# A decode step of two layers on one core: gate by three ScalarE functions, K slots freed by halves, a V head kept, priorities per batch

## The chip, the cores and the metric

One core of a Trainium2 chip. The metric is the device time of one execution of the whole program, in microseconds. Times on the chip come from the program's runs; the profile is one profiled execution.

## The reference, cut to what matters

```python
x = A_x                                            # [4, 1, 512], bf16
x = x + attention(layernorm(x), k_cache, v_cache, wq, wo)
x = x + ffn(layernorm(x), w_gate, w_up, w_down)
x = x + attention(layernorm(x), k_cache, v_cache, wq, wo)   # the same caches and weights again
x = x + ffn(layernorm(x), w_gate, w_up, w_down)

def attention(x, k_cache, v_cache, wq, wo):        # caches [4 batches, 8 heads, 4096, 128]
    q = (x @ wq)                                   # 32 query heads, 4 to a K/V head
    p = softmax(q @ k.T * 128 ** -0.5)
    return (p @ v) @ wo
def ffn(x, w_gate, w_up, w_down):                  # 512 -> 1792 -> 512
    return (gelu_tanh(x @ w_gate) * (x @ w_up)) @ w_down
```

All tensors are bf16. K and V are 32 heads each of 4096 x 128, 1.05 MB a head; the weights are some 13.9 MB. Both layers use the same caches and weights.

## The kernel before, in words

The two layers are called L = 0 and L = 1, the batches b = 0 to 3. The batches are independent of each other until the last step, so the kernel goes through the batches one after the other and does both layers of a batch on one load of its K heads. The weights are loaded once and stay in SBUF.

**Slots.** K and V heads come into `KV`, a tile of `SLOTS` = 12 slots, each for one head (128 partitions x 8 KB) or for two halves. Near the end the four parts of `wq_sb` serve as four more slots. A K head occupies its slot until the scores of layer 1 have used it. A V head is loaded once for each layer, except where `HELD` keeps it: for batches 1 to 3 head 7 stays from layer 0 to layer 1. The V loads of layer 1 go by halves (`HALVES`, 512 KB each), so that half a slot can be filled as soon as half a head has been used; a half is read by one of the two `values` steps of the head. K heads are loaded whole, and their slots come free when both halves of the scores are done.

**The steps of one batch.** K heads are transposed in place: heads 5 and 7 (`BY_PE`) by TensorE into `R_ps` with a copy by ScalarE (`kturn`, `kcopy`), the others by VectorE (`turn`, L366, two halves a head). `expand` (L392) spreads q into the weights `Qb`; `scores` (L415) makes the scores of four heads (z = 0 or 1) in two halves m of 16 matmuls; `top`, `bias`, `expo`, `pturn`, `pswap`, `pcopy` make the softmax's weights; `values` (L485) multiplies half a head of V, 16 matmuls; `oscale` scales. For layer 0 the dense chain of the batch follows: `outproj` (`proj`, `half_out`, `half_sum` L639, `proj_last` L623), `addback` (L646, L647), the norm (`ln_sq` L500, `ln_mm` L506, `ln_mid`, `ln_var`, `ln_root`), gate and up matmuls (`up`, L655), their transpose (`ffturn`, L662), the gate (`gelu_a`, `gelu_b` L688, `gelu_y`, `gelu_c` L705 to L707), `down` (L715), `addback`, the norm, and the q projection for layer 1 (`qmm` L538, `qevac` L551, `qturn` L556, `qsplit` L595, `qrep` L605). Only then can layer 1's scores of this batch run. The output projection of layer 1 is done once, for all four batches, after the last V head, and with the second FFN it makes the tail: `leave` (L732) adds and sends the output off.

The norm's factor 1/root is not applied to the norm's output but later: to q in the exponent's scale, and in the FFN to the gate's argument and to the product.

**The order.** `Plan` holds every step as a node with its engine, an estimated duration and what it depends on. `run` goes through time as a list scheduler: for each engine it takes the step that can begin first, with some `PATIENCE` for one of higher level that is ready a little later. The level is the longest path to the end, plus an offset by the kind of step (`LEAD`, `stage`). The loads go out on SP's queue in a fixed order: x, wq, K of batch 0, half of wo, V of batch 0, the rest of wo, w_gate, w_up, w_down, then for each batch b from 1 on K(b), V(b) for layer 0, V(b-1) for layer 1. Each waits on SP for a slot that its readers have left, and what stands behind it on SP waits too. `warm` puts filler matmuls (`spin`, L1004) before steps of TensorE that begin after an idle time. The whole order is computed when the program is built; on the chip nothing is chosen.

## Time and profile before

| | |
|---|---|
| time, median of 3 runs | 292.3 us (291.77 to 293.2) |
| the profiled execution's own time | 291.89 us |
| its span, first to last instruction | 290.1 us |
| granted clock of TensorE | 0.998 |
| busy: PE, DVE, ACT | 236.3, 133.5, 74.5 us |
| loaded by the load queue | 111.42 MB |

The page and the views give times in us from the span's start. L715 is line 715 of the kernel before. A row of a group or of the timeline has the engine, what is written and read, the shapes and how often; a row of the windows has the stretch, the busy time of each engine, the granted clock, the share of the sixteen DMA engines' time that packets took (over 1 where packets of one engine overlap) and the rate.

### The profile page before, as it was taken

What the parts mean: (1) busy time and instruction counts of PE and PEld (TensorE: products, weight loads), DVE (VectorE), ACT (ScalarE), POOL (GpSimd) and SP (SyncE); (2) the same over time, 40 slices, a digit from 0 to 9 for tenths busy, and PEclk for the clock granted to TensorE, in tenths of its full rate; (3) what the DMA queues carried; (4) which work ended last, traced back from release to release, by engine and by line L of the source; (5) the groups of instructions that cost most, each with busy time, mean ns of one, the idle gap of its engine ahead of it and who ended that gap; (6) DMA issues with size and microseconds to landing.
All of it is one profiled execution on the core that took longest, in us unless ns stands there. A gap on an engine that the chain in (4) does not pass through costs nothing.

```text
span 290.1 us, 9733 instructions
## 1 busy us (share of the span) xinstructions
PE 236.3 (81%) x4419; PEld 138.3 (48%) x4419; DVE 133.5 (46%) x380; ACT 74.5 (26%) x167; POOL 0.7 (0%) x6
## 2 busy tenths in 40 slices
PE   4988887878687888798888698879977889897794
PEld 1433454443233565455434465554445655565552
DVE  4149911002289942052389721343998213444034
ACT  1020751001023852101224731000338321113010
POOL 0000000000000000000000000000000000000000
PEclk9999999999999999999999999999999999999999
DMA  7999999999999999999999999999999999999910
GB/s 312 412 421 419 376 405 416 414 371 426 415 407 395 419 421 417 402 407 406 393 417 416 425 416 411 405 407 390 413 422 416 408 387 403 396 382 420 411 47 1
DMA packets 21657, 112.04 MB, mean 386 GB/s; under 512 B 2032, under 2 KB 6128, under 8 KB 12272
## 3 DMA queue, kind: packets, MB, share of 16 engines
q1 hardware_dynamic: 21568, 111.42, 95.3%
q8 instruction: 34, 0.56, 0.8%
q14 instruction: 7, 0.06, 0.0%
q10 hardware_dynamic: 48, 0.01, 0.0%
HBM read 111.42 MB, written 0.00 MB: 384 GB/s over the span
## 4 chain that ended last, share of the span: by engine, by line
DMA 62%; PE 16%; SPq 11%; DVE 7%; issue 2%; ACT 1%; DVEq 0%
DMA KV<-in_A_v_cache_dram 43%; DMA KV<-in_A_k_cache_dram 8%; SPq L351 7%; PE O_ps L485 7%; DMA wd_sb<-in_B_w_down_dram 6%; DMA wq_sb<-in_A_v_cache_dram 5%; SPq L741 3%; PE S_ps L415 3%; DVE KV L366 2%; PE R_ps L715 1%; PE R_ps L538 1%; DVE PA L662 1%; PE S_ps L1004 1%; PE R_ps L655 1%; DVE sm L421 1%
## 5 line engine op out<-in xcount | busy, mean ns | idle before, releaser
L485 PE MATMUL O_ps<-PA,KV 128*128 128x56 bf16 x1920 | 66.3, 188 | 20.8 <-DMA KV<-in_A_v_cache_dram 17.3
L485 PEld LDWEIGHTS <-KV 128*128 128x128 bf16 x1920 | 57.6, 97 | 40.8 <-DMA KV<-in_A_v_cache_dram 32.4
L1004 PE MATMUL S_ps<-iden_b 128*128 128x512 bf16 x226 | 67.7, 401 | 3.6 <-DVE iden_b L321 3.6
L366 DVE STREAM_TRANSPOSE KV<-KV 128x1024 int32<-128x1024 int32 x48 | 56.5, 1214 | 0.6 <-DMA KV<-in_A_k_cache_dram 0.4
L379 ACT ACTIVATE KV<-R_ps 128x512 bf16<-128x512 f32 x64 | 34.9, 595 | 28.0 <-PE R_ps L373 27.9
L415 PE MATMUL S_ps<-KV,PA 128*32 128x512 bf16 x384 | 35.3, 394 | 2.1 <-DVE KV L366 1.3
L1004 PEld LDWEIGHTS <-iden_b 128*128 128x128 bf16 x227 | 21.9, 107 | 27.6 <-issue 11.7
L373 PE MATMUL R_ps<-iden_b,KV 128*128 128x128 bf16 x256 | 22.1, 219 | 6.3 <-ACT KV L379 3.1
L421 DVE TENSOR_REDUCE sm<-S_ps 128x1 f32<-128x512 f32 x16 | 10.8, 677 | 27.4 <-PE S_ps L415 27.4
L373 PEld LDWEIGHTS <-KV 128*128 128x128 bf16 x256 | 15.8, 97 | 14.8 <-issue 10.2
L415 PEld LDWEIGHTS <-PA 128*32 128x32 bf16 x384 | 11.4, 94 | 13.2 <-issue 4.4
L493 DVE TENSOR_TENSOR OT<-O_ps,XS 128x4 bf16<-128x4 f32 (+1 forms) x12 | 2.0, 164 | 32.9 <-PE O_ps L485 32.9
L415 PE MATMUL S_ps<-KV,QN 128*32 128x512 bf16 x128 | 16.8, 381 | 0.2 <-ACT KV L379 0.2
L438 ACT ACTIVATE PA<-S_ps,sm 128x512 bf16<-128x512 f32 x16 | 11.7, 732 | 20.4 <-DVE sm L432 17.6
L632 ACT ACTIVATE PA<-R_ps 128x256 f32<-128x256 f32 x10 | 3.8, 384 | 46.2 <-PE R_ps L613 41.1
L529 ACT ACTIVATE sm<-sm 128x1 f32<-128x1 f32 (+1 forms) x10 | 2.0, 203 | 52.6 <-DVE sm L522 52.6
L493 DVE TENSOR_TENSOR OT<-O_ps,rdk 128x16 bf16<-128x16 f32 (+3 forms) x18 | 3.1, 170 | 26.7 <-PE O_ps L485 26.7
L463 ACT ACTIVATE PA<-T_ps 128x512 bf16<-128x512 f32 x16 | 9.6, 597 | 13.0 <-PE T_ps L455 11.8
L556 DVE STREAM_TRANSPOSE PA<-PA 128x256 int32<-128x256 int32 x10 | 4.4, 437 | 14.9 <-ACT PA L551 14.2
L613 PE MATMUL R_ps<-wo_sb,OT 128*1 128x512 bf16 (+1 forms) x124 | 8.7, 378 | 2.6 <-DMA wo_sb<-in_A_wo_dram 1.4
L646 DVE STREAM_TRANSPOSE PA<-R_ps 128x128 f32<-128x128 f32 x9 | 2.9, 317 | 16.5 <-PE R_ps L623 10.2
L447 DVE STREAM_TRANSPOSE PA<-PA 128x256 int32<-128x256 int32 x16 | 7.0, 434 | 7.5 <-ACT PA L438 7.5
(92 smaller groups left out, 173.9 us busy)
## 6 DMA issues: line engine op xcount, KB each, us to landing
KV<-in_A_v_cache_dram SPq DMA_DIRECT2D x34, 1024.0 KB, 15.0
KV<-in_A_k_cache_dram SPq DMA_DIRECT2D x32, 1024.0 KB, 13.5
KV<-in_A_v_cache_dram SPq DMA_DIRECT2D x46, 512.0 KB, 7.0
wq_sb<-in_A_wq_dram SPq DMA_DIRECT2D x1, 4096.0 KB, 12.2
wo_sb<-in_A_wo_dram SPq DMA_DIRECT2D x2, 2048.0 KB, 19.5
wq_sb<-in_A_v_cache_dram SPq DMA_DIRECT2D x4, 1024.0 KB
wg_sb<-in_B_w_gate_dram SPq DMA_DIRECT2D x1, 1792.0 KB
wu_sb<-in_B_w_up_dram SPq DMA_DIRECT2D x1, 1792.0 KB
```

The source lines that it names most:

```text
L351: nc.sync.dma_start(out=where[name], in_=src.rearrange("(p c) d -> p (c d)", p=P))
L366: nc.vector.transpose(out=w, in_=w)
L373: nc.tensor.matmul(R_ps[k % 2][:, P * u:P * u + P], lhsT=where[name][:, at:at + P], rhs=iden_b[:], start=True, stop=True)
L379: nc.scalar.activation(out=where[name][:, 512 * k:512 * k + 512], in_=R_ps[k % 2][:], func=ACT.Copy)
L415: nc.tensor.matmul(S_ps[z][32 * t:32 * t + 32], lhsT=w, rhs=k, start=(m == 0 and x == 0), stop=(m == 1 and x == 3))
L421: nc.vector.tensor_reduce(out=cms[:, z:z + 1], in_=S_ps[z][:].rearrange("p c r -> p (c r)"), axis=AX.X, op=ALU.max)
L438: nc.scalar.activation(out=PW[L][z].rearrange("p (a r e) -> p a r e", a=8, e=2), in_=S_ps[z][:].rearrange("p (a e) r -> p a r e", e=2), fu ...
L463: nc.scalar.activation(out=PW[L][z], in_=T_ps[z][:].rearrange("p t x -> p (t x)"), func=ACT.Copy)
L485: nc.tensor.matmul(Ov[L][:, j], lhsT=vw[:, c, :], rhs=w[:, c // 2, :, c % 2].unsqueeze(1).broadcast_to([P, WIDE, 4]), start=(m == 0 and c ...
L613: nc.tensor.matmul(R_ps[0][32 * i:32 * i + nb, :], lhsT=src[:, 4 * j + i, 0:nb], rhs=wo_sb[:, 4 * j + i, :], start=(first and j == heads[0 ...
L741: return lambda pick: nc.sync.dma_start(out=dst, in_=src.rearrange(pat, q=P))
L1004: nc.tensor.matmul(sinks[place].rearrange("p (a n) -> p a n", a=4), lhsT=iden_b[:], rhs=every, start=True, stop=True)
```

## The change

It has these parts:

- **V head 7 of batch 0 is kept** from layer 0 to layer 1 as in the other batches (`HELD`), and its two half loads of layer 1 are gone.
- **K slots come free by halves.** The two halves of a slot have readers of their own, for whole loads too: the first half of a K head is free after `scores` m = 0. K head 3 of batch 1 (`K_HALVES`) is loaded in two halves into the two halves of one slot.
- **Gate.** 1/(1 + e^u) was made by exp on ScalarE, then an add and a reciprocal on VectorE; now ScalarE does exp, ln(1 + .) and exp of the negative.
- **Norm.** The sums of x and of x² are two matmuls instead of one, so that the mean's doesn't wait for the squares.
- **q of layer 1, first half.** The matmuls write their columns in another order (`qmm_apart`), and VectorE transposes 512 fp32 columns in PSUM in place (`qturn_apart`) instead of ScalarE's copy and a bf16 transpose in SBUF.
- **The end.** The gate's matmuls and their transpose go in two parts of 8 and 6 of the 14 chunks (`CUT`, also for w_down's loads); the norm's factor is applied to the product's last rows in `leave` (`last_root`, `rrow`) and no more to the product; heads 4, 5, 6 are scaled one by one, and heads 5 and 6 take the narrow path of `proj_last`.
- **Order.** `LEAD` gets an offset for each batch and kind, `PATIENCE` depends on the kind of step, and some estimated durations change.

```diff
-HELD = ((), (7,), (7,), (7,))
-HALVES = {(b, 1, j) for b in range(3) for j in range(8)} | {(3, 1, 6)}
+HELD = ((7,), (7,), (7,), (7,))
+HALVES = {(b, 1, j) for b in range(3) for j in range(7)} | {(3, 1, 6)}
+K_HALVES = {(1, 3)}
-PATIENCE = (0.5, 1.5, 0.7)
-LEAD = {"tn1": -3, "val0": 1, "sc10": -2, "chain": 2, "sc11": -6, "sm00": 1, "os0": -6, "op": -2, "sm01": 11, "sm10": 10, "qx1": 4, "other": 5, "sc00": 2, "sm11": 8, "os1": -4, "tn0": -2, "sc01": 1}
+PATIENCE = (0, 11.7, 5.1, 7.5, 0)
+LEAD = {"chain": (26.5, 10.5, 23.5, 46.5), "end": (-35, -36.5, -45.5, -72), "kt1": (3.5, -7, -16.5, 24),
...
+        "sm11": (1, 15, 57.5, 62), "tn0": (-47.5, -37, -37.5, -45.5), "tn1": (-60.5, -107.5, -79, -91),
+        "val0": (-95.5, -54.5, -70.5, -63.5), "val1": (0, 13, 33.5, -23)}
-WARM = 0.45
+WARM = 0.4
...
                 if v["readers"] is not None:
-                    slot_rd[pick] = v["readers"]
+                    mate = pick
                     whole[pick[0]] = not v["half"]
-                    if not v["half"]:
-                        slot_rd[pick[0], 1] = v["readers"]
+                    if v["half"]:
+                        slot_rd[pick] = v["readers"]
+                    else:
+                        slot_rd[pick[0], 0], slot_rd[pick[0], 1] = v["readers"]
...
+    def ln_place(s, nb):
+        return O_ps[0][:, 512 - CD * nb:] if s else R_ps[1][:, 0:CD * nb]
+
+    def ln_mm(s, bs, nb):
+        def emit():
+            st = ln_place(s, nb).rearrange("p (k b) -> p k b", k=CD)
+            nc.tensor.matmul(st, lhsT=ones_mean, rhs=XS[:, s, :, bs], start=True, stop=True)
+        return emit
...
+    def qturn_apart():
+        nc.vector.transpose(out=R_ps[0][:], in_=R_ps[0][:])
...
+    def last_root():
+        nc.vector.scalar_tensor_tensor(out=junk, in0=rs, scalar=1.0, in1=pick_b, op0=ALU.mult, op1=ALU.mult,
+                                       accum_out=rrow)
...
             nc.scalar.activation(out=u, in_=u, func=ACT.Exp, scale=-2.0 * GELU_C * GELU_A)
+            nc.scalar.activation(out=u, in_=u, func=ACT.Ln, bias=1.0)
+            nc.scalar.activation(out=u, in_=u, func=ACT.Exp, scale=-1.0)
...
             else:
-                nc.vector.tensor_tensor(out=g, in0=g, in1=y.unsqueeze(1).broadcast_to([P, CF, nb]),
-                                        op=ALU.mult)
                 nc.vector.tensor_tensor(out=g, in0=g, in1=d, op=ALU.mult)
...
-    def gelu_c(nb):
-        def emit():
-            d, g, u, h = ff(nb)
-            nc.vector.tensor_scalar(out=u, in0=u, scalar1=1.0, scalar2=1e30, op0=ALU.add, op1=ALU.min)
-            nc.vector.reciprocal(out=u, in_=u)
+    def gelu_h(nb):
+        def emit():
+            _, g, u, h = ff(nb)
             nc.vector.tensor_tensor(out=h, in0=g, in1=u, op=ALU.mult)
...
-        nc.vector.tensor_tensor(out=yo, in0=xrow, in1=R_ps[0][:, 0:P], op=ALU.add)
+        nc.vector.scalar_tensor_tensor(out=yo, in0=R_ps[0][:, 0:P], scalar=rrow, in1=xrow, op0=ALU.mult, op1=ALU.add)
...
-            g = [[7], [6, 5, 4], [3, 2, 1, 0]] if b < B - 1 else [[0], [1, 2, 3], [7], [4, 5], [6]]
+            g = [[7], [6, 5, 4], [3, 2, 1, 0]] if b < B - 1 else [[0], [1, 2, 3], [7], [4], [5], [6]]
...
+            rd = [[("sc", b, 1, j // 4, m)] for m in range(2)]
+            if (b, j) in K_HALVES:
+                for m in range(2):
+                    if j >= 3:
+                        soft = [("sc", b - 1, 1, 0 if j < 7 else 1, m)]
+                    pl.load(name + (m,), 4.15, ld_part(name, m, src), rd[m], soft=soft, half=True)
+            else:
+                pl.load(name, 8, ld_head(name, src), rd, soft=soft)
...
-        a = add(("lnq", tag), "DVE", 0.17, [after], ln_sq(bs, nb))
-        a = add(("lnm", tag), "PE", 0.4, [a], ln_mm(bs, nb), ins=4)
-        a = add(("lnc", tag), "DVE", 0.37, [a], ln_mid(bs, nb))
-        v = add(("lnv", tag), "DVE", 0.33, [a], ln_var(nb))
+        s = add(("lnq", tag), "DVE", 0.17, [after], ln_sq(bs, nb))
+        m = add(("lnm", tag), "PE", 0.35, [after], ln_mm(0, bs, nb), ins=4)
+        a = add(("lnc", tag), "DVE", 0.3, [m], ln_mid(bs, nb))
+        s = add(("lns", tag), "PE", 0.35, [s, m], ln_mm(1, bs, nb), ins=4)
+        v = add(("lnv", tag), "DVE", 0.45, [s, a], ln_var(nb))
...
+            if not z and not root:
+                after = add(("qm", tag, z), "PE", 1.1, [after], qmm_apart(bs), ins=32)
+                last = add(("qt", tag, z), "DVE", 0.72, [after], qturn_apart)
+                last = spread_q(b, 1, z, last, "apart")
+                continue
...
+            for k in range(2):
+                u1 = add(("up", tag, 0, k), "PE", (0.55, 0.45)[k], [a, u1], up(0, wg_sb, bs, nb, k), ins=32)
+                t0 = add(("ft", tag, 0, k), "DVE", (0.44, 0.36)[k], [u1, t0], ffturn(0, k))
...
+    p, y = parts(B - 1, 1), rs
+    a = outproj(("op", "last"), p, len(p) - 2, 1, al, B, [dense_end], [])
+    r = add("rz", "DVE", 0.1, [("os", B - 1, 1, i) for i in range(len(groups(B - 1, 1)))], rows_clear)
+    w, a = a, ln(("f", "last"), a, al, B, y)
+    r = add("rp", "DVE", 0.2, [w, r], rows)
+    r = add("ro", "DVE", 0.45, [r, ("lnv", ("f", "last"))], rows_turn)
+    a = ffn("last", a, al, B, y)
+    y = add("rr2", "DVE", 0.16, [("lnr", ("f", "last")), ("gh", "last")], last_root)
+    add("out", "DVE", 0.32, [a, r, y], leave)
```

More of the change, by code (lines that the diff above doesn't have):

```diff
@@ L607, in qrep, with proj @@
         return emit
-    def proj(src, nb, heads, first, last):
+    def proj(src, cols, nb, heads, first, last):
         def emit():
@@ L616, in proj, with proj_last @@
         return emit
-    def proj_last(src, nb, heads, last):
+    def proj_last(src, cols, nb, heads, last):
         def emit():
```

184 lines of the change are left out of this document (100 added, 84 removed), and 4 rows, old and new, of the table LEAD.

## The prediction

> **What bounds the kernel now.** I read the page first (share of each engine, the DMA line, the sizes of the loads), then the stretches (busy time, DMA share and GB/s of chosen windows), then the DMA queue's waits and its timeline, and last the chain of waits for the two places where something other than the stream decides.
>
> ```profile
> PE 236.3 (81%) x4419; PEld 138.3 (48%) x4419; DVE 133.5 (46%) x380; ACT 74.5 (26%) x167; POOL 0.7 (0%) x6
> GB/s 312 412 421 419 376 405 416 414 371 426 415 407 395 419 421 417 402 407 406 393 417 416 425 416 411 405 407 390 413 422 416 408 387 403 396 382 420 411 47 1
> q1 hardware_dynamic: 21568, 111.42, 95.3%
> L1004 PE MATMUL S_ps<-iden_b 128*128 128x512 bf16 x226 | 67.7, 401 | 3.6 <-DVE iden_b L321 3.6
> KV<-in_A_v_cache_dram SPq DMA_DIRECT2D x46, 512.0 KB, 7.0
> ...
> 104.00:110.00 6.00, 4.91 (x112) 3.65 (x112) 1.13 (x2) 2.17 (x4) 0.00 (x0) 1.00 1.02 419
> 184.00:194.00 10.00, 8.50 (x251) 5.84 (x248) 4.71 (x22) 0.62 (x3) 0.00 (x0) 1.00 1.02 407
> ```
>
> PE is 81% busy, but 67.7 us of its 236.3 are L1004, the filler matmuls of `spin`; without them it works some 169 us of 290, and DVE and ACT less. The load queue moves 111.42 MB and keeps the sixteen engines at 95.3% of the span, and the GB/s line stays between 371 and 426 from the second slice to the 38th. So the stream of loads bounds the kernel: it ends near 276 us, and a tail of dependent steps follows. What a change is worth is bytes, gaps in the stream, and the tail. In a stretch of whole heads (1024 KB each) the stream runs at 419 GB/s, in one of half heads (512 KB) at 407, both at a DMA share of 1.02: halves cost 3% of rate and no idle time.
>
> The one gap lies between batch 0 and batch 1:
>
> ```profile
> 86.00:87.00 1.00, 1.00 (x26) 0.53 (x19) 1.00 (x2) 0.18 (x1) 0.00 (x0) 1.00 0.87 360
> 87.00:88.00 1.00, 0.94 (x5) 0.30 (x4) 0.90 (x6) 0.00 (x0) 0.00 (x0) 1.00 0.75 287
> 88.00:89.00 1.00, 0.28 (x5) 0.17 (x4) 0.68 (x3) 0.87 (x2) 0.00 (x0) 1.00 0.96 369
> ...
> 65.98 0.33 SPq L351 DMA_DIRECT2D KV<-in_A_k_cache_dram  x1
> KV<-in_A_k_cache_dram SPq DMA_DIRECT2D x1, 1024.0 KB, 23.3
> 86.42 3.08 SPq L351 DMA_DIRECT2D KV<-in_A_k_cache_dram  x4
> 84.39 2.02 PE L415 MATMUL S_ps<-KV,PA 128*32 128x512 bf16 x32 [0.21 <-DVE PA L392]
> ```
>
> The fourth K head of batch 1 is issued at 65.98 and lands 23.3 us later, at 89.3. The next load is issued at 86.42, when the 32 matmuls of layer 1's first scores (heads 0 to 3) end: only they free a slot. Three windows fall under 1.02 by 0.15, 0.27 and 0.06, so 0.48 us of stream is lost here.
>
> **The change part by part.**
>
> *Bytes.* V head 7 of batch 0 stays in its slot for both layers, so two half loads go: 1.05 MB at 407 GB/s = 2.58 us. K head 3 of batch 1 goes from 419 to 407: 1.05 x (1/407 - 1/419) = 0.07 us more. Net -2.5.
>
> *The gap.* The held head takes the slot that K head 3 had at 65.98, so only three K heads are queued ahead, and the stream runs dry 1.05 MB / 419 = 2.5 us earlier. Against that, halves of a slot are freed: K head 3's first half may go after 16 of the 32 score matmuls, 2.02 / 2 = 1.0 us earlier than 86.42. And the chain to these scores changes:
>
> ```profile
> 78.90 0.59 PE R_ps L715 x28
> 80.07 0.18 DVE XS L500
> 80.29 0.40 PE R_ps L506 x2
> 82.22 0.61 ACT PA L551
> 82.85 0.46 DVE PA L556
> 81.38 1.25 DVE L366 STREAM_TRANSPOSE KV<-KV 128x1024 int32<-128x1024 int32 x1
> ```
>
> It starts when w_down has landed (the bytes ahead of it are the same). Its last part has 24 matmuls instead of 28: 0.59 x 4/28 = -0.08. The mean's matmul no longer waits for the squares: from 80.29 to where the squares began, 80.07, -0.22; the second matmul and its reduction lie beside the q projection. For q's first half, ACT's copy and DVE's bf16 transpose (0.61 + 0.46 and a hop of 0.02) become one DVE transpose of 512 fp32 columns in PSUM. The tail's row at 282.79, quoted below, has 448 columns in 0.66, so an estimate is 0.75, and -0.34. Sum -0.64, if DVE is free: the K transpose of 81.38 ran to 82.63 under the cover of ACT's copy. The new transpose would be ready near 81.95; behind that K transpose it starts at 82.65, ends at 83.40 and not 83.31, and the three gains come to +0.1. I take -0.5, since the order is made anew from priorities that rank the chain over K transposes. So the refill comes 0.9 to 1.6 earlier than 86.42; I take 1.5, near 84.9.
>
> What that does to the stream's end: behind the refill stand the same bytes in both kernels (K head 3 has moved behind it, a V head has left). DMA engines that run dry in both kernels therefore end earlier by what the refill moved, 1.5; those that don't, by the full 2.5. The 0.48 us over two microseconds show that not all are dry at once; I take 7 in 10 for the new gap: 2.5 - 0.7 x (2.5 - 1.5) = 1.8. Bounds: 0.9 (all dry, no gain of the chain) and 2.5 (no further loss).
>
> The new wait stands on SP's queue: K head 3 waits there for the first half of the scores, and behind it K heads 4 to 7 and the V heads, which need these scores or later ones anyway. From its issue at 86.42 until the share is back at 0.96 pass 1 to 1.5 us. That delay is in both kernels and cancels; only if the second half, issued 1.0 after the first, leaves a hole of its own does it cost again (a rival below). The Trainium skill speaks against halving here: "DMA: Bandwidth & Descriptors", under "Anatomy of one DMA" (there for the GpSimd path), gives each DMA a fixed cost of about 2.0 us beside its bytes, which for one more DMA would turn the bytes' -2.5 into -0.5. At 184 to 194 us the trace does not show such a charge: other loads move meanwhile.
>
> *Slots later on.* Of the four slots freed by the last scores before 91.85, K head 7 takes one that a V head had; V head 3 of batch 1 follows on V head 7's last use, which layer 1 makes first. Batches 1 and 2 run so today, and their stretches show no gap like the one above. Cost 0, covered by some 5 us of loads in flight; thin, since the queue's waits have
>
> ```profile
> SPq L357 <- PE O_ps L485: 22.5, 27, 2.0
> ```
>
> 27 half loads that waited for PE to free a slot. Where a new order frees them late by more than is in flight, the stream loses it one for one: 0 to 2.5 us, nothing taken.
>
> *The dense chains of batches 1 to 3* shorten as batch 0's. They don't end the stream; 0. *The larger leads and patience* reorder PE, DVE and ACT; where the stream covers them, 0.
>
> *The tail* after the last landing is on the path:
>
> ```profile
> 278.46 0.34 PE R_ps L639 x4
> 278.80 0.54 PE O_ps L485 x16
> 279.73 0.29 PE R_ps L623 x16
> 280.68 0.17 DVE XS L500
> 280.97 0.41 DVE PA L728
> 281.81 0.96 PE R_ps L655 x16
> 282.79 0.66 DVE PA L662
> 284.05 0.22 DVE PA L681
> 284.26 0.56 DVE PA L662
> 284.82 0.11 DVE PA L697
> 284.95 0.22 DVE PA L699
> 285.17 0.12 DVE PA L705
> 285.31 0.52 DVE PA L706
> 285.85 0.23 DVE PA L707
> 286.12 0.98 PE R_ps L715 x56
> 287.12 0.29 DVE PA L732
> 284.30 0.25 ACT L688 ACTIVATE PA<-PA 128x56 f32<-128x56 f32 x1 [1.80 <-DVE PA L681]
> ```
>
> - Half sums: today L639 at 278.46 stands between the two halves of the last head. With heads 5 and 6 both in the last part they come earlier: 0 to -0.34, taken -0.2. Head 5's own 16 narrow matmuls (0.29 by L623) run before the last half lands.
> - Norm: the squares (0.17 and gaps, -0.2) leave the path, and the rows' transpose (280.97, 0.41) goes behind the variance, so that it doesn't take the place that the squares left.
> - Gate matmuls and transpose in two parts: the first part's transpose (256 of 448 columns, 0.38) runs beside the second part's matmuls; then 192 columns, 0.28, behind matmuls that end as before at 282.77 or 0.1 later for twice as many instructions. 0.66 becomes 0.3 to 0.5; -0.2.
> - Gate: today from ACT's start at 284.30 to the end of L707 at 286.08. After: ACT has three steps, 3 x 0.25 + 2 x 0.02 = 0.79, to 285.09; DVE beside it the second transpose to 284.82 and one product (0.22, L697 is gone) to 285.06. The last product then ends at 285.09 + 0.05 + 0.23 = 285.37: -0.71. The last root, one step on four columns, lies beside the 0.98 of L715, and L732's successor keeps its 0.29.
>
> The row of 0.25 is the price I use for each ACT step. The Trainium skill, "ScalarE: Activation LUTs", under "Rules for kernel authors", would budget about 0.3 us and 0.83 ns an element for each: 1.04 for three by my estimate, and the gate would bring 0.46. The row doesn't agree with it, by 0.1 a step.
>
> Sum of the tail: -0.2 - 0.2 - 0.2 - 0.7 = -1.3; from -0.7 (no gain from order and split, 0.5 from the gate) to -1.7.
>
> **Sum.** The profiled execution took 291.89 us (span 290.1), 0.4 under the median of 292.3. 291.89 - 1.8 - 1.3 = 288.8; its own bounds are 287.7 (2.5 and 1.7) and 290.3 (0.9 and 0.7). I forecast 288.8.
>
> **The rivals.**
>
> *The gap adds nothing.* The chain gains enough, or enough DMA engines are late, that all 2.5 arrives: 291.89 - 2.5 - 1.3 = 288.1. For it: the stream never fell under 0.75 in a window. Against it: 2.5 us less is queued, and the refill gains at most 1.6.
>
> *A later stall gives part back.* The waits above show V slots freed late in the half-head stretches; 1 to 2.5 us lost there gives 289.8 to 291.3.
>
> *Slower: K transposes ahead of the dense chain.* In batch 0, DVE has six transposes of 1.25 us for the three landed K heads (L366). If the new order puts them ahead of the chain to layer 1's scores, every microsecond by which the first half of those scores ends later than 85.4 moves the refill, and with it the stream's end. The change breaks even when the refill comes 1.3 us later than 86.42, the tail's gain; it is 0.5% slower from 1.3 + 1.5 = 2.8 us later, three of these transposes beyond the lost 1.0. With all six in front (7.5 us, less the 1.0): 291.89 + 6.5 - 1.3 = 297; with four 294.6. Against it: today one such transpose ran there, in a hole of the chain.
>
> *A hole between the halves.* The first half is 0.52 MB, 1.3 us at 407. If a load into a dry queue takes its 1 to 1.5 us anew and the second half comes late, the hole is up to 1.0: 289.8. The Trainium skill's fixed cost (above) would make it 2.0, and 290.8. Against it: the halves' issues lie 1.0 apart, less than 1.3.
>
> *The bytes don't count.* If something else than the stream held the end, only the tail's -1.3 is left: 290.6. The GB/s line speaks against it.
>
> **How the numbers follow.** A measurement of this kernel can tell about 0.5% from no change, 1.46 us: under 290.4 is faster, over 293.4 slower. The forecast has 0.49, the gap that adds nothing 0.16, the later stall 0.13, the hole 0.04, the slower order 0.10, the bytes that don't count 0.08. Faster: the first two whole, the hole, and 0.07 of the stall, 0.49 + 0.16 + 0.04 + 0.07 = 0.76. Same: 0.04 of the stall, the 0.08, and 0.01 of the slower order that stays small: 0.13. Slower: 0.09 of the order and 0.02 of a stall over 4 us: 0.11. The range leaves out the slower order and the far ends: 287.4 to 291.5; the likeliest case alone is 287.7 to 290.3.
>
> **What would show it.** Right: queue bytes down by 1.05 MB; a dip of the DMA share near 84 to 87 us, deeper than today's, with the next K load issued near 85; the stream's end 1.8 us earlier; from the last V matmul to L732's counterpart 1.1 us less; three ACT steps of about 0.25 in the gate. Wrong: the same end of the stream in spite of fewer bytes, a second dip after 100 us, K transposes on DVE between w_down's landing and the scores, or ACT steps over 0.4.

## The result, and the profile after

The changed kernel takes 295.08 us (median of 11 runs, 293.98 to 299.97), the kernel before 292.78 us in runs beside it. The ratio is 1.0093, interval [1.0065, 1.0120]: 0.9% or 2.7 us slower, where 3.1 us less were forecast. A few executions of either kernel are longer at a lower clock; the ratios leave them out and so are not quite the quotient of the medians. The profiled execution of the changed kernel took 297.44 us (span 295.6, granted clock 0.977), 2.4 over its median. So its trace shows where time goes; how much a part costs is taken from the ratios below.

The page of the kernel after; columns as before:

```profile
PE 233.0 (79%) x4428; PEld 142.8 (48%) x4428; DVE 133.5 (45%) x383; ACT 74.6 (25%) x173; POOL 0.7 (0%) x6
PEclk9999999999999979999999799999989999999979
GB/s 315 408 425 418 371 412 415 408 385 419 415 278 371 419 421 401 364 390 401 349 412 417 421 391 369 374 390 396 386 421 423 413 413 407 400 405 417 361 14 2
q1 hardware_dynamic: 21424, 110.37, 93.5%
L1078 PE MATMUL S_ps<-iden_b 128*128 128x512 bf16 x182 | 56.0, 412 | 3.6 <-DVE iden_b L343 3.6
```

The 1.05 MB are gone (110.37 against 111.42), and yet the stream ends later. Slice 12, at 81 to 89 us, fell from 407 to 278 GB/s: that is the forecast gap, but deeper. Slices 17 to 20 and 24 to 29 stand at 349 to 401, where before had 390 to 416: a second loss, a stall after 100 us. The clock row has four slices at 7 or 8 where before had none, and there are 182 fillers where there were 226.

How the stream falls behind is seen best by adding up the packets of the load queue in the trace: the time at which so many MB have arrived, in before, and by how much each kernel is later (one profiled execution each; labels as in the experiments).

| MB | before, us | after | e4 | e12 | e18 | e5 | e15 | e10 |
|---|---|---|---|---|---|---|---|---|
| 32 | 80.7 | 0.0 | 0.0 | 0.2 | 0.0 | 0.1 | 0.2 | 0.0 |
| 36 | 91.0 | 2.7 | 2.6 | 3.5 | 2.7 | 0.9 | 0.1 | 0.8 |
| 44 | 110.2 | 2.7 | 2.5 | 3.5 | 2.7 | 1.3 | 0.1 | 0.8 |
| 52 | 129.7 | 4.1 | 2.7 | 3.5 | 3.4 | 1.3 | 0.8 | 1.1 |
| 60 | 149.9 | 5.0 | 2.4 | 3.4 | 3.2 | 1.2 | 0.7 | 1.3 |
| 76 | 188.4 | 6.8 | 2.5 | 3.5 | 3.3 | 1.8 | 0.8 | 1.3 |
| 92 | 227.8 | 7.4 | 2.8 | 3.9 | 3.3 | 1.9 | 1.0 | 3.3 |
| 108 | 268.3 | 6.3 | 1.5 | 2.7 | 2.7 | 2.4 | 1.1 | 6.5 |

A kernel that keeps the head has 1.05 MB less to load in all, 2.5 us: with a lag of 2.5 it is level. After reaches that lag by 36 MB, in the gap behind batch 0, and loses some 4 us more between 44 and 76 MB. How much is lost there differs from trace to trace: summed in the same way, three other kernels with the new order (e17, e1, e8) lose 1.1, 1.4 and 2.0 us between 44 and 76 MB, and four with the old order and the kept head (e6, e18, e3, e7) 0.0, 0.6, 1.2 and 1.8. So the table shows where this execution lost its time; what a part costs is read from the ratios. Its last byte arrives at 281.83, before's at 278.00.

The profiled execution's 5.55 us over before are then: the last byte 3.83 later; from there to the transpose behind the last projection 4.16 instead of 2.12 (+2.04); from that transpose to the end of the last add 6.61 instead of 7.29 (-0.68); the way out +0.32; outside the span +0.05.

### The profile page after: what moved, and what is told of

It reads as the page before. It is cut to its first block, busy times and chain, and to the rows that moved or that the text cites. A ratio compares the mean times of both kernels' runs of the same rounds, so it can differ in the third digit from the quotient of the medians.

```text
span 295.6 us, 9761 instructions
## 1 busy us (share of the span) xinstructions
PE 233.0 (79%) x4428; PEld 142.8 (48%) x4428; DVE 133.5 (45%) x383; ACT 74.6 (25%) x173; POOL 0.7 (0%) x6
## 3 DMA queue, kind: packets, MB, share of 16 engines
q1 hardware_dynamic: 21424, 110.37, 93.5%
HBM read 110.37 MB, written 0.00 MB: 373 GB/s over the span
## 4 chain that ended last, share of the span: by engine, by line
DMA 59%; PE 22%; SPq 10%; DVE 5%; issue 3%; ACT 0%; DVEq 0%
DMA KV<-in_A_v_cache_dram 45%; PE O_ps L507 9%; DMA KV<-in_A_k_cache_dram 8%; SPq L373 6%; DMA wd_sb<-in_B_w_down_dram 6%; PE S_ps L437 6%; SPq L795 3%; PE R_ps L395 1%; DVE sm L443 1%; PE R_ps L662 1%; PE R_ps L708 1%; PE R_ps L767 1%; PE R_ps L578 1%; DVE PA L716 0%; ACT PA L485 0%
## 5 line engine op out<-in xcount | busy, mean ns | idle before, releaser
L507 PE MATMUL O_ps<-PA,KV 128*128 128x56 bf16 x1920 | 67.5, 191 | 17.6 <-DMA KV<-in_A_v_cache_dram 14.5
L507 PEld LDWEIGHTS <-KV 128*128 128x128 bf16 x1920 | 60.0, 98 | 34.9 <-DMA KV<-in_A_v_cache_dram 24.3
L1078 PE MATMUL S_ps<-iden_b 128*128 128x512 bf16 x182 | 56.0, 412 | 3.6 <-DVE iden_b L343 3.6
L388 DVE STREAM_TRANSPOSE KV<-KV 128x1024 int32<-128x1024 int32 x48 | 55.9, 1210 | 0.6 <-DMA KV<-in_A_k_cache_dram 0.5
L395 PE MATMUL R_ps<-iden_b,KV 128*128 128x128 bf16 x256 | 23.1, 228 | 10.1 <-DMA KV<-in_A_k_cache_dram 5.6
L1078 PEld LDWEIGHTS <-iden_b 128*128 128x128 bf16 x188 | 18.0, 107 | 23.5 <-issue 9.8
L395 PEld LDWEIGHTS <-KV 128*128 128x128 bf16 x256 | 17.0, 102 | 18.0 <-issue 9.8
L437 PEld LDWEIGHTS <-PA 128*32 128x32 bf16 x384 | 12.0, 94 | 16.6 <-issue 8.0
L515 DVE TENSOR_TENSOR OT<-O_ps,rdk 128x4 bf16<-128x4 f32 (+2 forms) x19 | 3.3, 171 | 18.4 <-PE O_ps L507 18.3
L469 DVE STREAM_TRANSPOSE PA<-PA 128x256 int32<-128x256 int32 x16 | 7.0, 435 | 8.6 <-ACT PA L460 8.6
L490 PEld LDWEIGHTS S_ps<-mask_th,sm 128*128 128x128 f32 x32 | 5.1, 196 | 10.6 <-ACT PA L460 9.6
```

The source lines that it names most:

```text
L388: nc.vector.transpose(out=w, in_=w)
L395: nc.tensor.matmul(R_ps[k % 2][:, P * u:P * u + P], lhsT=where[name][:, at:at + P], rhs=iden_b[:], start=True, stop=True)
L437: nc.tensor.matmul(S_ps[z][32 * t:32 * t + 32], lhsT=w, rhs=k, start=(m == 0 and x == 0), stop=(m == 1 and x == 3))
L507: nc.tensor.matmul(Ov[L][:, j], lhsT=vw[:, c, :], rhs=w[:, c // 2, :, c % 2].unsqueeze(1).broadcast_to([P, WIDE, 4]), start=(m == 0 and c ...
L1078: nc.tensor.matmul(sinks[place].rearrange("p (a n) -> p a n", a=4), lhsT=iden_b[:], rhs=every, start=True, stop=True)
```

## The experiments

Each ratio is to the kernel before, run on the same chip, with its 95% interval. Every kernel is planned anew when it is built, so one edit can move steps far from it.

### The kept head, alone and with the halves

Theory: the slot taken away dries the queue and costs what the bytes save. Rival: it gains 1.8 us, as forecast, and something else loses it. e4 is the kernel before with the head kept:

```diff
-HELD = ((), (7,), (7,), (7,))
-HALVES = {(b, 1, j) for b in range(3) for j in range(8)} | {(3, 1, 6)}
+HELD = ((7,), (7,), (7,), (7,))
+HALVES = {(b, 1, j) for b in range(3) for j in range(7)} | {(3, 1, 6)}
```

> The kernel before with V head 7 of batch 0 kept and nothing else. Slot theory: 2.5 us of bytes are saved, and the gap near 86 us grows by about 2.5 us since the fourth K head waits for all 32 score matmuls: ratio 0.998 to 1.003. If the held head costs nothing: ratio 0.991. If the one slot less also stalls the V loads of batch 0: over 1.004.

e12 adds the slots freed by halves and K head 3 in two loads:

```diff
 (e4, and)
+K_HALVES = {(1, 3)}
-                    if not v["half"]:
-                        slot_rd[pick[0], 1] = v["readers"]
+                    if v["half"]:
+                        slot_rd[pick] = v["readers"]
+                    else:
+                        slot_rd[pick[0], 0], slot_rd[pick[0], 1] = v["readers"]
...
```

> The kernel before with V head 7 of batch 0 kept, K slots free by halves and K head 3 of batch 1 in two loads; steps, priorities and threshold as before. Against the run with the kept head alone (1.0002): the first half of K head 3 goes 1.0 us earlier, before's chain has no K transpose ahead of the expansion of q, so the gap is about 1 us smaller: ratio 0.996 to 0.997. If the hole between the halves takes it: 1.000.

Measured: e4 1.0002 [0.9982, 1.0022], e12 1.0006 [0.9980, 1.0033]. The kept head nets nothing, and the halves add nothing. The windows show where the time goes (stretch; length; busy PE, PEld, DVE, ACT, POOL; clock, DMA share, GB/s). Those of after:

```profile
85.00:86.00 1.00, 1.00 (x24) 0.50 (x20) 0.97 (x3) 0.00 (x0) 0.00 (x0) 1.00 0.42 156
86.00:87.00 1.00, 1.00 (x21) 0.46 (x14) 0.54 (x2) 0.00 (x0) 0.00 (x0) 1.00 0.08 20
87.00:88.00 1.00, 0.41 (x2) 0.00 (x0) 1.00 (x3) 0.00 (x0) 0.00 (x0) 1.00 0.92 340
88.00:89.00 1.00, 0.94 (x20) 0.58 (x23) 0.93 (x5) 0.25 (x1) 0.00 (x0) 1.00 0.75 234
```

The windows of e4:

```profile
86.00:87.00 1.00, 1.00 (x29) 0.50 (x22) 1.00 (x2) 0.03 (x1) 0.00 (x0) 1.00 0.00 0
87.00:88.00 1.00, 1.00 (x5) 0.29 (x3) 0.90 (x4) 0.15 (x1) 0.00 (x0) 1.00 0.53 90
88.00:89.00 1.00, 0.25 (x5) 0.19 (x4) 0.78 (x4) 0.80 (x2) 0.00 (x0) 1.00 0.66 246
89.00:90.00 1.00, 0.88 (x26) 0.71 (x26) 0.90 (x4) 0.07 (x1) 0.00 (x0) 1.00 1.06 451
```

The windows of e12:

```profile
87.00:88.00 1.00, 1.00 (x12) 0.42 (x7) 0.93 (x3) 0.18 (x1) 0.00 (x0) 1.00 0.83 303
88.00:89.00 1.00, 0.28 (x2) 0.09 (x1) 0.90 (x5) 0.65 (x1) 0.00 (x0) 1.00 0.69 254
89.00:90.00 1.00, 0.86 (x22) 0.72 (x21) 0.74 (x3) 0.22 (x2) 0.00 (x0) 1.00 0.74 250
90.00:91.00 1.00, 1.00 (x32) 0.58 (x24) 1.00 (x4) 0.60 (x1) 0.00 (x0) 1.00 1.09 307
91.00:92.00 1.00, 1.00 (x24) 0.57 (x16) 1.00 (x2) 0.00 (x0) 0.00 (x0) 1.00 0.90 287
92.00:93.00 1.00, 1.00 (x8) 0.44 (x6) 1.00 (x2) 0.21 (x1) 0.00 (x0) 1.00 0.95 311
```

The next K loads (start, length of the group) in the timeline of SP's queue; in after:

```profile
85.93 1.58 SPq L379 DMA_DIRECT2D KV<-in_A_k_cache_dram  x2
```

in e4:

```profile
86.61 2.03 SPq L351 DMA_DIRECT2D KV<-in_A_k_cache_dram  x4
```

and in e12:

```profile
85.83 1.46 SPq L363 DMA_DIRECT2D KV<-in_A_k_cache_dram  x2
```

In e4 the share goes to 0.00: all sixteen engines ran dry, not "7 in 10". The load that refills them is issued at 86.61, no earlier than before's 86.42, and the same bytes stand behind it; so the end cannot come earlier. Added up from 84 to 93 us, the stream lacks 0.59 us of its 419 GB/s in before, 3.23 in e4, 3.27 in after: 2.6 lost for 2.5 saved. In e12 the first half goes out 0.78 earlier, at 85.83, and data come a microsecond earlier (303 GB/s at 87 to 88 against 90), but then the rate stays at 250 to 311 until 93, where e4 is back at 451 by 90. The stream lacks 3.76 there: the early issue is lost on the way back to full rate. That is not for want of loads: the second half follows 0.94 behind the first, three whole heads are issued by 88.34, and from 88 to 92 some 2.9 to 3.6 MB are issued and not yet landed (issues less packets ended, added up from the trace). Nor is it a hole between the halves. In these microseconds 4 KB packets took 174 to 194 ns on average (163 at 184 to 194 us in before) and the 8 KB packets behind them 608, 419 and 399 ns, where e4's took 309 from 89 on; why is not settled. The Trainium skill's fixed cost for each DMA ("DMA: Bandwidth & Descriptors", "Anatomy of one DMA"), which the prediction set beside its sum, does not explain this: e4 issues two DMAs fewer than before and loses 2.6, e12 issues one more than e4, and their ratios differ by 0.0004.

e2 looks at the same part in the kernel after (e6, below, with the old order). It is after without the kept head and without K head 3's halves:

```diff
-HELD = ((7,), (7,), (7,), (7,))
-HALVES = {(b, 1, j) for b in range(3) for j in range(7)} | {(3, 1, 6)}
+HELD = ((), (7,), (7,), (7,))
+HALVES = {(b, 1, j) for b in range(3) for j in range(8)} | {(3, 1, 6)}
-K_HALVES = {(1, 3)}
+K_HALVES = set()
```

> The changed kernel without the kept V head of batch 0 and without the K head in two loads; all else as changed (K slots still free by halves). Slot theory: the gap at 84 to 90 us shrinks from 2.6 to about 0.5 us of stream, which pays for the 2.5 us of bytes that come back: ratio within 0.3% of the changed kernel's 1.009. Order theory: the same here, and the later stalls (some 4 us between 112 and 215 us) stay. Clock theory: the same, with the clock still near 0.97.

1.0109 [1.0059, 1.0159], not to be told from after's 1.0093: without the kept head the loss is there as well.

### The order

Theory: the new `LEAD` and `PATIENCE`, priced at 0, lose the time. Rival: they are neutral. On the side of after, e3 takes all of the order back, and e18 the leads alone:

```diff
 (e3; e18 has the LEAD lines only)
-DMA_FETCH = 0.8
+DMA_FETCH = 1.5
-PATIENCE = (0, 11.7, 5.1, 7.5, 0)
-LEAD = {"chain": (26.5, 10.5, 23.5, 46.5), ...
+PATIENCE = (0.5, 1.5, 0.7, 0.5, 0.5)
+LEAD = {"tn1": -3, "val0": 1, "sc10": -2, "chain": 2, ...
```

> The changed kernel with the priorities, the patience and the fetch cost of before's planner; steps, kept head, halves and filler threshold as changed. Order theory: the stream loses its 4 us between 112 and 215 us no more, ratio about 0.995. Clock theory: clock dips stay and with them most of the loss, ratio 1.005 or more. Slot theory: only the gap at 84 to 90 us stays (2 us), ratio about 1.000.

> The changed kernel, all of it, with before's priorities (patience, fetch cost, threshold, steps, kept head as changed). If the priorities per batch are the loss beside the kept head's gap: ratio 0.999 to 1.004, as with priorities and patience of before (1.0026). If they fit the changed steps and kept head, and hurt only before's: 1.009 or more.

On the side of before, e10 puts the whole new order on the old steps, e13 the patience alone, e14 the leads alone:

```diff
 (e10; e13 has PATIENCE and its use only, e14 LEAD and its use only)
-DMA_FETCH = 1.5
+DMA_FETCH = 0.8
-PATIENCE = (0.5, 1.5, 0.7)
-LEAD = {"tn1": -3, "val0": 1, "sc10": -2, "chain": 2, ...
+PATIENCE = (0, 11.7, 5.1, 7.5, 0)
+LEAD = {"chain": (26.5, 10.5, 23.5, 46.5), ...
```

> The kernel before with the changed priorities per batch, patience and fetch cost of the planner, and nothing else. Order theory: the stream loses 3 to 5 us between 112 and 215 us, ratio 1.005 to 1.015. If the order only hurts together with the kept head or the new steps: 1.000 within 0.3%.

> The kernel before with the planner's new patience alone (old priorities). If the patience (no waiting for a more urgent step, except ahead of K transposes) makes the order's 2%: ratio 1.012 to 1.025. If the priorities per batch make it: 1.000 within 0.4%.

> The kernel before with the new priorities per batch alone (old patience). If the priorities make the order's 2%: ratio 1.012 to 1.025, V loads of batch 3 issued late near 227 and 243 us as with both. If the patience makes it: 1.000 within 0.4%. If only both together: each under 1.008.

| kernel | ratio to before | interval |
|---|---|---|
| after | 1.0093 | [1.0065, 1.0120] |
| e3, after with the old order | 1.0026 | [0.9995, 1.0057] |
| e18, after with the old leads | 1.0031 | [1.0011, 1.0050] |
| e10, before with the new order | 1.0215 | [1.0185, 1.0246] |
| e13, before with the new patience | 1.0029 | [1.0003, 1.0054] |
| e14, before with the new leads | 1.0552 | [1.0494, 1.0610] |

The order is the largest part of the loss, and of the order the leads: taking them back in after gives 0.62%, 1.8 of the 2.7 us, with intervals that do not touch; what e3 takes back beside them, patience and `DMA_FETCH`, changes no more there. A second pair says the same: e1 (after with the old filler threshold, below) and e6 (the same with the old order as well, below) differ in the order alone, 1.0055 against 0.9999, with intervals that just meet. The mean granted clock is not the difference: it is 0.976 over the runs of after that its ratio counts and 0.978 over those of e18.

How an order loses time is plainest in e10. Its windows, and rows of VectorE's and TensorE's timeline (start, length):

```profile
210.00:214.00 4.00, 0.00 (x0) 0.00 (x0) 4.00 (x4) 0.00 (x0) 0.00 (x0) 0.50 1.02 426
218.00:222.00 4.00, 3.57 (x44) 1.98 (x45) 2.13 (x4) 3.44 (x8) 0.00 (x0) 0.50 1.01 420
228.00:230.00 2.00, 1.97 (x48) 1.77 (x48) 1.97 (x3) 1.94 (x4) 0.00 (x0) 1.00 0.56 131
242.00:244.00 2.00, 2.00 (x58) 1.45 (x47) 0.00 (x0) 0.60 (x1) 0.00 (x0) 1.00 0.46 193
...
207.51 8.10 DVE L381 STREAM_TRANSPOSE KV<-KV 128x1024 int32<-128x1024 int32 x7
215.76 0.24 PE L620 MATMUL T_ps<-qs,fold_b 128*32 128x64 bf16 x4 [9.23 <-DVE qs L610]
```

and its queue's waits (queue and line, what it waited for: us in total, times, longest):

```profile
SPq L366 <- PE O_ps L500: 34.4, 19, 15.9
SPq L372 <- PE O_ps L500: 28.1, 26, 5.8
```

VectorE turns seven half K heads, 8.10 us, ahead of the split of q for which TensorE waits 9.23 us. At 210 to 214 us TensorE has nothing to do, and the granted clock is 0.50. At 218 to 222 TensorE is busy again, 3.57 of 4 us, still at half clock. The V heads are then used late and the slots come free late (15.9 us for one whole head and 5.8 for one half load; the longest such waits in before are 4.6 and 2.0), and at 228 and 242 the DMA engines are only about half busy: the lag in the table goes from 1.3 to 6.5 us between 76 and 108 MB. How much of this is the idle stretch and how much the half clock behind it is not measured apart.

The Trainium skill, "TensorE: Matmul & The Clock Gate", Part 1, has the clock fall to half after an idle window of about 3.4 us and come back only after such a window of work. On the way back these traces agree, on the way down they ask for less than an idle window. The clock record of each trace moves in steps of 3.41 us. Counted in windows of that length over the twenty traces, it falls to half 42 times before the last microseconds of the span, behind windows in which TensorE was busy for 0.56 to 2.54 us; every window with less than 1.49 us of work at full clock was followed by half clock. It comes back 42 times, always behind a window with 3.05 us of work or more; seven windows with 2.92 or less left it at half.

In e14 the loss comes in batch 1, at 108 to 114 us (its profiled execution is 2.3 over its median):

```profile
104.00:106.00 2.00, 1.80 (x12) 1.12 (x11) 0.00 (x0) 1.82 (x5) 0.00 (x0) 0.50 1.02 410
110.00:112.00 2.00, 1.39 (x6) 0.42 (x6) 1.62 (x6) 0.51 (x1) 0.00 (x0) 1.00 0.04 16
112.00:114.00 2.00, 1.68 (x35) 0.90 (x35) 0.70 (x2) 0.86 (x3) 0.00 (x0) 1.00 0.00 0
```

K transposes go ahead again: VectorE does seven from 95.10 to 103.09, and TensorE, at half clock from 97.04 to 107.28, does those of heads 5 and 7 before it replicates q at 107.09. Batch 1's first scores start at 107.94, and no load is issued between 93.45 and 115.19, when the first V slot comes free (in before between 93.27 and 103.89); the queue ran dry on the way.

In after the loss is spread, and no single wait stands out. One stretch, the window in after:

```profile
144.00:148.00 4.00, 3.62 (x71) 2.43 (x71) 3.77 (x15) 1.45 (x5) 0.00 (x0) 1.00 0.96 324
```

and the same window in e18, with the old leads:

```profile
144.00:148.00 4.00, 3.41 (x52) 1.88 (x47) 3.43 (x14) 1.46 (x5) 0.00 (x0) 1.00 1.00 406
```

The share is nearly the same and the rate is not: the 8 KB packets took 387 ns on average in after and 321 in e18 (medians 312 and 313), because some were slow (one in ten over 589 ns, in e18 over 321). That a queue with little in it makes packets slower does not fit: the loads issued and not yet landed grew from 2.0 to 4.9 MB in these 4 us, in e18 from 2.7 to 4.2. What slows single packets stays open, and so does how much of after's loss is made of it.

### The new steps without the order, and the K transposes in the chain

Theory: in the chain to layer 1's first scores, VectorE now takes a K transpose of 1.23 us while q waits. Rival: the chain comes out 0.5 shorter, as forecast. e5 is after with the old order, the old filler threshold and no kept head, so that the new steps stand alone; e15 is e5 with batch 1's K transposes made to wait for batch 0's q; e17 puts that wait into after:

```diff
 (e15 against e5, e17 against after)
-add(("tn", b, j, m), "DVE", 1.22, [("k", b, j, m) if (b, j) in K_HALVES else ("k", b, j)],
+add(("tn", b, j, m), "DVE", 1.22, [("k", b, j, m) if (b, j) in K_HALVES else ("k", b, j),
+                                   ("qx", 0, 1, 0) if b == 1 else None],
```

> The changed kernel's steps (gate by three ScalarE functions, split norm, q in PSUM, end in two parts, K slots free by halves), but with the priorities, patience, fetch cost and filler threshold of before, V head 7 of batch 0 loaded twice and K head 3 whole. Order and slot theories together: no gap beyond before's, no later stall; the tail's last steps (from the transpose of the last projection to the last add) take 6.6 us and not 7.3: ratio 0.996 to 0.999. If the new steps themselves slow the stream (a K transpose between q's spreading and its expansion at 83 us): ratio 1.002 or more.

> The new steps with the old order and no kept head (1.0061), and with batch 1's K transposes held back until q's first half of layer 1 is expanded. If the K transpose in the chain's 0.5 us hole is what the new steps cost: first scores some 1 us earlier, the gap at 87 us under 0.5 us of stream, ratio 0.998 to 1.002. If the new steps cost elsewhere (V slots of batch 2 and 3): over 1.004.

> The changed kernel, all of it, with batch 1's K transposes held back until q's first half of layer 1 is expanded. If the transpose in the chain is the main loss of the changed kernel: first scores near 84.1 instead of 84.8, ratio 1.002 or less against its 1.009. If the order's later stalls are the main loss: a gain of 0.7 us or less, ratio 1.006 to 1.009.

Timeline rows of VectorE and TensorE (start, length), in after:

```profile
83.04 0.22 DVE L644 TENSOR_TENSOR qs<-R_ps,sm 128x64 bf16<-128x64 f32 x1
83.18 1.23 DVE L388 STREAM_TRANSPOSE KV<-KV 128x1024 int32<-128x1024 int32 x1
84.34 0.38 DVE L414 TENSOR_TENSOR PA<-T_ps,sm 128x256 bf16<-128x256 f32 x1
84.78 2.06 PE L437 MATMUL S_ps<-KV,PA 128*32 128x512 bf16 x32 [0.25 <-DVE PA L414]
```

The same rows of e15:

```profile
83.04 0.23 DVE L638 TENSOR_TENSOR qs<-R_ps,sm 128x64 bf16<-128x64 f32 x1
83.58 0.42 DVE L408 TENSOR_TENSOR PA<-T_ps,sm 128x256 bf16<-128x256 f32 x1 [0.32 <-PE T_ps L648]
84.06 2.02 PE L431 MATMUL S_ps<-KV,PA 128*32 128x512 bf16 x32 [0.20 <-DVE PA L408]
```

In after VectorE has nothing of the chain to do for the half microsecond in which TensorE replicates q, and into this hole the plan puts a K transpose of 1.23 us. Scores start at 84.78, 0.39 later than in the kernel before (84.39); in e15, with the wait, they start at 84.06, 0.33 earlier than there. Measured: e5 1.0061 [1.0031, 1.0090], e15 0.9970 [0.9942, 0.9999]: 0.9%. That is 2.7 us, more than the 0.75 by which e5's scores (84.81) start after e15's. The table has 1.2 of it by 44 MB, behind the gap; the rest comes later, where the plans differ too. In after the wait (e17) gives 1.0067 [1.0042, 1.0093], which after's interval does not exclude, although it brings what the prediction had counted on. Two rows of e17, of TensorE and of SP's queue:

```profile
83.93 2.08 PE L437 MATMUL S_ps<-KV,PA 128*32 128x512 bf16 x32
85.03 1.76 SPq L379 DMA_DIRECT2D KV<-in_A_k_cache_dram  x2
```

The scores start 0.46 earlier than in before, and the refill goes out at 85.03, 1.39 earlier. Yet between 84 and 93 us the stream lacks 2.31 us (by its windows, as above), 1.7 more than in before: of the 2.5 saved 0.8 are left.

e6 is e5 with the kept head and the halves, e7 is e6 with the wait:

> As the run before it, with V head 7 of batch 0 kept and K head 3 in two loads. Slot theory: the gap near 86 us loses about 2.5 to 3.5 us of stream, the bytes give 2.5 back: within 1 us of the run without the kept head, ratio 0.996 to 1.003. Clock theory: against the earlier run with the old order and threshold 0.4 (1.0026) the clock comes back over 0.99 and about 1 us is gained.

> As the run before it, with one more dependency: VectorE may not transpose batch 1's K heads before q's first half of layer 1 is expanded. If the K transpose of 1.23 us in the 0.5 us hole of the chain delays the first scores and so the refill of the dry queue: first scores 0.7 us earlier, first K half issued 0.7 earlier, ratio 0.002 to 0.003 under the run before. If the refill's time does not set the stream's end: the same ratio.

0.9999 [0.9969, 1.0028] and 0.9984 [0.9945, 1.0022]. Here the kept head takes 0.6% off e5 and adds 0.1% to e15, so the two do not add up: with both, the queue is dry in any case and an earlier start of the scores moves only the refill. In e7 the lag at 36 MB falls to 2.0, from e6's 3.8, and a new lag of 1.7 comes at 52 to 56 MB. What each edit is worth depends on the plan around it; this part I cannot split further.

### The tail

e9 puts only the gate by three ScalarE steps, with one product, and the last root on the final rows into the last FFN of before; e16 adds the norm in two matmuls there:

```diff
+            if nb > 1:
+                nc.scalar.activation(out=u, in_=u, func=ACT.Ln, bias=1.0)
+                nc.scalar.activation(out=u, in_=u, func=ACT.Exp, scale=-1.0)
...
-        nc.vector.tensor_tensor(out=yo, in0=xrow, in1=R_ps[0][:, 0:P], op=ALU.add)
+        nc.vector.scalar_tensor_tensor(out=yo, in0=R_ps[0][:, 0:P], scalar=rrow, in1=xrow, op0=ALU.mult, op1=ALU.add)
```

> The kernel before with the changed gate, root and last add in the last FFN only (three ScalarE steps, one product, the root on the final rows). If the tail's arithmetic was right: the chain from the last ScalarE exp to the last product 0.7 us shorter, all before it as it was, ratio 0.9975. If the stream moves too with any new plan: the ratio differs from that by over 0.3%.

> The kernel before with the changed gate, root and last add and the split norm in the last FFN only, the order before it as it was. Against the same without the norm (0.9961): 0.2 us more in the chain of the end, ratio 0.994 to 0.997, and under before's time beyond its interval. If a new plan moves the stream: more than 0.3% away from that.

Measured: e9 0.9961 [0.9934, 0.9988], 291.88 us: faster than both kernels by this interval, though short of the 0.5% bound. e16 is 0.9976 [0.9953, 0.9999], not to be told from e9. The gate in after, by ScalarE's timeline:

```profile
290.10 0.25 ACT L742 ACTIVATE PA<-PA 128x56 f32<-128x56 f32 x1 [1.88 <-DVE PA L735]
290.66 0.25 ACT L744 ACTIVATE PA<-PA 128x56 f32<-128x56 f32 x1
```

rows of after's chain of waits:

```profile
287.45 1.05 PE R_ps L708 x32
288.52 0.72 DVE PA L716 x2
289.34 0.23 DVE PA L732
289.85 0.22 DVE PA L735
290.06 0.57 DVE PA L716
290.65 0.23 DVE PA L753
290.97 0.23 DVE PA L759
291.25 0.98 PE R_ps L767 x56
292.25 0.35 DVE PA L786
```

and ScalarE's timeline in e9:

```profile
284.53 0.25 ACT L688 ACTIVATE PA<-PA 128x56 f32<-128x56 f32 x1 [1.79 <-DVE PA L681]
285.09 0.25 ACT L691 ACTIVATE PA<-PA 128x56 f32<-128x56 f32 x1
```

From ScalarE's first step to the end of the last product are 290.10 to 291.20 in after and 284.53 to 285.64 in e9 (by its chain), where before had 284.30 to 286.08.

### The filler threshold

The change also lowers `WARM` from 0.45 to 0.4, which the prediction did not price. e1 and e8 are after with 0.45 and 0.7, e11 is before with 0.4:

```diff
 (e1; e8 has 0.7; e11 is the reverse in before)
-WARM = 0.4
+WARM = 0.45
```

> The changed kernel with the filler threshold of before (WARM 0.45, not 0.4); the order of all other work is the same. Clock theory (fewer filler matmuls, 182 instead of 226, let the granted clock fall to 0.76-0.83 in places, so that PE frees V slots late and is slow in the tail): granted clock back over 0.99, 2 to 3 us faster than the changed kernel, ratio to before about 1.000. Order theory (the new priorities free V slots late) and slot theory (the held head opens the gap at 84 to 90 us): within 0.5 us of the changed kernel, ratio about 1.008.

> The changed kernel with a filler threshold of 0.7 instead of 0.4, order of all other work the same. Clock theory: clock 0.99 or more throughout, and what is left over before is the order's and the slot's: ratio 1.003 to 1.006, span close to the run with 0.45 (1.0055). If the clock explained all: ratio 0.995 to 1.000. If filler delays real work: over 1.008.

> The kernel before with the changed filler threshold, 0.4 instead of 0.45; the order of all other work is the same. Clock theory: granted clock falls from 0.998 to 0.96 to 0.98, ratio 1.002 to 1.004. If the order and not the threshold made the dips: clock over 0.99, ratio within 0.2% of 1.000.

1.0055 [1.0023, 1.0088], 1.0060 [1.0023, 1.0096] and 0.9994 [0.9969, 1.0018]. On before's steps the threshold costs nothing; in after the 0.4% that 0.45 seems to give lies inside overlapping intervals, and 59 fillers more than after's 182 (e8) give no more. With the old order the same step, e3 against e6, is 0.3%, again within the intervals. What a half clock costs at the end is seen in after's profiled execution, in its last windows:

```profile
278.00:280.00 2.00, 0.86 (x22) 0.54 (x19) 0.17 (x1) 0.00 (x0) 0.00 (x0) 1.00 0.84 334
282.00:284.00 2.00, 2.00 (x36) 1.49 (x36) 0.17 (x1) 0.77 (x2) 0.00 (x0) 0.50 0.00 0
```

TensorE is busy 0.86 of 2 us at 278 and then runs the last V matmuls at half clock. From the last byte to the transpose behind the last projection it is 4.16 us here, and 1.95 to 2.10 in e1, e2 and e3. By the rows of the chain, against the same steps in e1, the half clock makes 1.3 of the 2.04 us above. That the lower threshold brings it about is not shown: e11 has such a stretch with 0.4 too (0.50 at 278 to 280), e2 and e18 with 0.4 have none there, and e8, with the most fillers, has one at 274.46. How often it happens no run here shows.

## Why the prediction was wrong, point by point

- **The order, taken at 0.** This step and the next failed by some 1.8 us each. "Where the stream covers them, 0" assumed what was to be shown: that slots still come free in time. The prediction's own row had 27 half loads that waited for PE, with "nothing taken" for it. Measured: 0.62% (1.8 us) for the leads in after, 0.6 to 0.7% for the whole order in two pairs, 2.15% for the new order on the old steps. It is the rival "a later stall", at 0.13; its price of 1 to 2.5 us holds the 1.8, but its 289.8 to 291.3 still counted on the gap's gain. On the old steps (e10, e14) the mechanism is that of the rival "slower", K transposes ahead of the chain, in batches that it did not look at. A half clock behind stretches with little work for PE was in no case of it.
- **The gap: -1.8 forecast, 0.0 measured (e4).** The text had the right argument, that behind the refill stand the same bytes, so engines that run dry in both kernels gain only what the refill gains. It failed in the "7 in 10" and in the 1.5 of the refill: the share goes to 0.00 to 0.08, so it is 10 in 10, and the refill came 0.5 earlier in after, 0.2 later in e4. Its lower bound of 0.9 had left out that the refill gains nothing. And it took the stream to be at its rate once refilled: in e17 the refill came 1.4 earlier, and 0.8 were left in place of 1.4 or more.
- **Halves: 1.0 from half scores.** Issued 0.5 to 0.8 earlier, yes, and useless. The rival "a hole between the halves", at 0.04, has about the size of the loss but not its form: the second half came in time (0.94 behind the first), and from 88 to 93 us the stream ran at 250 to 311 GB/s though whole heads were queued behind it. What makes a refill by halves slower than one by whole heads is open. The -0.5 that the prediction set beside its sum, for one more DMA, left out that the kept head takes two away.
- **The chain: -0.5.** It was +0.39 in after, -0.33 with the wait in e15 and -0.46 with the wait in after (e17), so the sum was right and the condition "if DVE is free" failed. The working had found the K transpose that could take the place (bound +0.1) and set it aside because priorities rank the chain higher. It slipped in one step later, behind q's split. That is the mechanism of the slower rival in small: one transpose, not four.
- **The tail: -1.3 forecast, -0.68 in the trace from the last projection on.** Gate: -0.71 forecast; 1.10 instead of 1.78, -0.68 by the ends above, and e9 confirms it alone. The 0.25 held for each ScalarE step, against the Trainium skill's budget ("ScalarE: Activation LUTs", "Rules for kernel authors") that would have made it 0.35. (The 0.46 that the prediction gave for the gate by that budget left out the two hops of 0.02; it is 0.42.) Norm: from the end of the add behind the last projection to the gate's matmuls 0.93 instead of 1.17, -0.24; forecast -0.2. Split of gate and transpose: -0.2 forecast, +0.16 measured (1.89 instead of 1.73): the two transposes ran one behind the other, 0.72, after all 32 matmuls (1.05), and nothing was hidden; why the first did not start beside the second part isn't settled. Half sums: no gain seen; two of them still stand among the last V matmuls. The last add has 0.35 instead of 0.29: the factor on the rows isn't free, +0.06.
- **Right:** the bytes (110.37 MB), the stream as the bound (in before its last byte lands at 278.0, not near 276), the dip at 84 to 87 us, ScalarE's steps, the gate. Two of the signs it named for being wrong are there: a second dip after 100 us, and a K transpose between w_down's landing and the scores.
- **The sum by what the runs show.** Three kernels lead from before to after. The new steps with the kept head and the halves, in the old order and with the old threshold (e6), are at 0.9999 [0.9969, 1.0028]: 0.0 us, where -3.1 were forecast. The lower threshold brings 1.0026 (e3), +0.8 us, within the intervals; the new order brings 1.0093, +2.0 us, with intervals that do not touch. In e6's 0.0 the gate and root are -1.1 (e9, 0.39% of 292.8; its interval allows 0.4 to 1.9) and the kept head and halves about 0 on before's steps (e4, e12). What takes the 1.1 back is not told apart: the K transpose in the chain (e7, with the wait, is at 0.9984; without the kept head the wait is worth 0.9%, e5 against e15) and the split are the candidates.

## What to carry to other kernels

Taking away a buffer ahead of a dependent refill saves no time by its bytes when the queue then runs dry: the end moves with the refill, so ask when the refill is issued, not how much less is loaded. In a kernel whose loads wait for slots a new set of priorities has to be priced like any other edit: by the slots that it frees later than what is in flight covers, and by the stretches in which it leaves TensorE little to do, since half clock follows them. Shortening a chain helps only if the hole it leaves is too short for the planner to fill with something long.

## What the runs showed of the hardware

- A load queue that ran dry comes back slowly: in e4 90 GB/s, then 246, then 451 in the three microseconds from 87 on, the load having been issued at 86.61. Refilled by two half heads first, e12 stayed at 250 to 311 until 93, with 2.9 to 3.6 MB issued and not landed from 88 to 92.
- A DMA share near 1 is not full rate: 324 GB/s at 0.96 in after, 406 at 1.00 in e18, by 8 KB packets of 387 and 321 ns on average, with 2.0 to 5.3 and 2.7 to 5.0 MB issued and not landed.
- TensorE's half clock outlasts the idle time: 0.50 at 218 to 222 us in e10 with 3.57 of 4 us busy.
- It needs no idle window: in after the four falls before the end, at 107.77, 165.80, 213.58 and 281.85 us, came behind 3.41 us in which TensorE had been busy for 1.48, 1.62, 1.66 and 1.73.
